# The product with v for the last 64 query rows of each batch: two heads as one 128-column weight tile

## The chip, the cores and the metric

The kernel runs on one core of one Trainium2 chip. The metric is the device time of one execution in microseconds (us); the time before is the median of three runs.

## The reference

Three stages follow one another. The attention has 4 batches of 8 heads, 576 tokens and a head width of 64; its scores get a decay from cumulated logarithms of f, and a causal mask. Its output, 2304 tokens of 512 columns, goes through a first feed-forward network (512 to 2048 to 512), and then through a routed one in which every token goes to one of eight experts.

```python
scores = scale * np.matmul(q, k.transpose(0, 1, 3, 2))
scores = np.where(causal, -1000000000.0, scores + decay)
attn = np.exp(scores - np.max(scores, axis=-1, keepdims=True))
attn = attn / (np.sum(attn, axis=-1, keepdims=True) + 1e-09)
out = np.matmul(attn, v)
x = out.transpose(0, 2, 1, 3).reshape(B * S, H * D)
h = x @ w_in
x = (h * np.clip(h + 3.0, 0.0, 6.0) / 6.0) @ w_out
# then per token: one of eight experts, relu(x @ w1[e]) @ w2[e], scaled by two gates
```

## The kernel before

Every fp32 operand is split into a high part (fp16) and a low part (bf16), and a product is three products: high by high, high by low, low by high.

**Attention.** The 576 queries of a batch and head are four blocks of 128 rows and a last one of 64 rows. The work comes in units. A "q" unit is one head and one or two blocks of 128 rows. A "t" unit is the last 64 rows of two heads: its scores fill 128 PSUM partitions, head e in partitions 64e to 64e+63, and its exponentials are transposed by a DMA into pt, where columns 64e to 64e+63 of each 128-column block belong to head e. There are four t units a batch, sixteen in all. `pv_unit` multiplies pt by v: pt is the weight operand, v (64 columns high, a column of ones, 64 columns low) the moving one, and the row sums come out as column 64 of the result. A q unit does it with 128 weight columns (L386 to L388). A t unit does it head by head with 64 weight columns each, both heads into PSUM partitions 0 to 63: per head four key blocks by three products (L396 to L398), and for the last 64 keys, whose high and low parts lie in the two halves of one block, L399 and L400, the latter with 64 rows of weights only: 28 matmuls a unit.

The results of one pair of heads share one PSUM bank (tile pv, one buffer). For the third group of rows of a batch the bank holds the fourth block of 128 rows of two heads (columns 0 to 129) and the t unit (columns 130 to 259). `evac` divides by the row sums on VectorE (L408 to L410), then ScalarE makes the high part in xn (L413) and GpSimd the low one (L414). The next user of the bank waits for the last read of it.

The scores of a t unit also use 64 weight columns: per head two matmuls of 512 columns in `scores` (L262) and two of 64 columns (L322, L323).

**First feed-forward.** Six chunks of 384 tokens; per chunk 192 matmuls of 384 columns in its first product (L634) and 192 in the second (L657). While a chunk is multiplied, the attention of later rows goes on between its matmuls: `adv` gives the attention a higher priority, and the order on TensorE is laid by the scheduler, matmul by matmul. After each chunk come 36 matmuls of 16 columns for the gates (L722). The last chunk waits for the end of the attention; the loads of the experts' weights (tile stw) begin after it too, as they take its room.

**Begin.** `setup` fills constants by GpSimd, the column of ones of v among them (L115). `prep_v` makes the two parts of v, block by block; of the last 64 tokens it loads two copies, one in each half of the partitions, and splits both.

Of the kernel before, what the change touches and what calls it, by code (L numbers as in the profile page):

```python
# [7 lines left out]
F16 = mybir.dt.float16  # L8
# [10 lines left out]
P = 128  # L19
PSC = 8.0        # PSUM units of a score: sqrt(D)  # L20
QW = [128, 256, 384, 512]

# the order of the work
# priority of the attention
ATTN_FIRST = 200
# priority of the conversion of the first feed-forward's weights
CONV_FIRST = 500
# share of a chunk's steps over which the next chunk's attention is spread
PACE = 0.75
# steps of the first chunk before the attention goes on  # L30
LEAD = 2
# units between the scores and the product with v
LAG = 4
# units between finished rows and their transposition
XLAG = 2
# units before the third and the fourth piece of the first batch
AT2, AT3 = 0, 4
# units of a group before the next pieces' preparation (Q2 rotates: at least 4)
PA, PB = 4, 4
# units before a batch's end at which the next one's first piece is prepared  # L40
PN = 2
# tiles of 64-bit floats of w_out in flight, and those in g before it is used
RAW_BUFS, RAW_G = 2, 3
# step of the attention from which w_out is loaded
WO_STEP = 12
# tiles converted and loaded before the first chunk
EARLY_CONV, EARLY_LOADS = 18, 22
# pieces of q and k split by DVE
DVE_PIECES = 2
# of four: parts of g that GpSimd splits in the first chunk  # L50
POOL_G = 4
# loads of w_in at points of the beginning
AHEAD = (1, 2, 1, 1, 1)
# the block of rows of the first batch after whose transposition later loads queue
# [4 lines left out]
def attention_moe_kernel(ctx: ExitStack, tc: tile.TileContext, q, k, v, f, w_in, w_out,  # L59
# [10 lines left out]
    SIZES = [3, 3, 3, 3, 3, 3]     # blocks of 128 tokens in a chunk  # L70
    NCH = len(SIZES)
    FIRST = [sum(SIZES[:c]) for c in range(NCH + 1)]    # a chunk's first block
# [45 lines left out]
    cumd = dram.tile([15, B * H, P], F16, name="cumd")      # (part, block of columns), row, column  # L118
# [26 lines left out]
    # columns of K: for four heads the even and the odd tokens of each 256, and the last 64 tokens of all heads  # L145
# [7 lines left out]
    def spare(i):  # L153
        """room in g, free until the first feed-forward begins"""
        return gf[:, i * 1024:(i + 1) * 1024]
# [8 lines left out]
    def piece(i):  # L164
        """the i-th piece of k or q: 256 tokens (two to a partition) of four heads, or a batch's last 64 tokens:
        batch, rows, heads, shape of a row's tile, columns of K"""
        b, n = i // NTB, i % NTB
        if n == 4:
            return b, 64, slice(0, H), (H, 1), slice(512, 576)
        g, hh = n // 2, n % 2  # L170
        return b, 128, slice(hh * 4, hh * 4 + 4), (4, 2), slice(g * 256, g * 256 + 256)

    def load(i, which):
        """the i-th piece of k or q, or the i-th block of 128 (or 64) tokens of v"""
# [22 lines left out]
    def load_cum(b, hh):  # L197
        """the parts of the cumulated decay of four heads, or of the last 64 tokens"""
# [7 lines left out]
    def split_kq(nm, i):  # L206
        """hi and lo parts of a piece (of q: lo and hi), side by side, for the transposition"""
# [37 lines left out]
    def q_cols(b, h, qb):  # L245
        """columns of q of a block of 128 tokens (the even ones, then the odd ones) or of the last 64"""
        if qb == 4:
            return [t[:, h, 0:64] for t in q_t[b * NTB + 4]]
        g, half = qb // 2, qb % 2
        return [t[:, half * 4 + h % 4, :] for t in q_t[b * NTB + g * 2 + h // 4]]  # L250

    def scores(ps, h, qb, l1, l2):
        """scores of a block of queries, by the parity of the key's token: [parity, pair]"""
# [10 lines left out]
    def pairs(t):  # L264
        """a row of keys in the order of the tokens, by their parity"""
# [13 lines left out]
    def prep_v(b, tb):  # L279
        if b * NTB + tb > 2:  # L280
            load(b * NTB + tb, "v")
        tv, V = ld.pop((b * NTB + tb, "v")), vt[b % len(vt)]
        nc.scalar.activation(out=V[:, tb, :, 0:64], in_=tv, func=AF.Copy)
        nc.gpsimd.tensor_tensor(out=V[:, tb, :, 65:129].bitcast(BF16), in0=tv, in1=V[:, tb, :, 0:64], op=ALU.subtract)

    # units: ("q", b, h, (qb, ...)) or ("t", b, hp): rows of the last 64 tokens of two heads
# [46 lines left out]
    def soft(u):  # L333
# [19 lines left out]
        if u[0] == "q" and u[1] == 0 and u[3] != (3,):  # L353
            # TensorE has nothing else to do before the first feed-forward
# [18 lines left out]
    def pv_unit(u, o, slot):  # L373
        """one unit into its columns of the bank o"""
# [15 lines left out]
        else:  # L390
            for e in range(2):
                h = u[2] * 2 + e
                oc = o[0:64, slot[e]:slot[e] + 65]
                cs = slice(e * 64, e * 64 + 64)
                for kb in range(4):
                    nc.tensor.matmul(oc, lhsT=pt[:, kb, cs], rhs=V[:, kb, h, 0:65], start=kb == 0, stop=False)  # L396
                    nc.tensor.matmul(oc[:, 0:64], lhsT=pt[:, kb, cs], rhs=V[:, kb, h, 65:129].bitcast(BF16), start=False, stop=False)
                    nc.tensor.matmul(oc, lhsT=ptb[:, 4 + kb, cs], rhs=V[:, kb, h, 0:65], start=False, stop=False)  # L398
                nc.tensor.matmul(oc, lhsT=pt[:, 8, cs], rhs=V[:, 4, h, 0:65], start=False, stop=False)  # L399
                nc.tensor.matmul(oc[:, 0:64], lhsT=pt[0:64, 8, cs], rhs=V[0:64, 4, h, 65:129].bitcast(BF16), start=False, stop=True)  # L400

    def evac(o, r, n, dests, h0):
        """o[0:r, n*2, 65] -> normalised, split, into dests (one [P, 2, H, D] tile per q block)"""
# [8 lines left out]
        for i, xt in enumerate(dests):  # L412
            nc.scalar.activation(out=xt[0:r, 0, h0:h0 + 2], in_=xs[0:r, 2 * i:2 * i + 2], func=AF.Copy)  # L413
            nc.gpsimd.tensor_tensor(out=xt[0:r, 1, h0:h0 + 2].bitcast(BF16), in0=xs[0:r, 2 * i:2 * i + 2],  # L414
                                    in1=xt[0:r, 0, h0:h0 + 2], op=ALU.subtract)

# [24 lines left out]
    def finish(n):  # L441
        """the transposition of finished rows, some units after them"""
# [8 lines left out]
    def pv(u):  # L451
# [10 lines left out]
        else:  # L462
            pv_unit(u, cur["o"][:, 130:512], [0, 65])
            evac(cur["o"], 128, 1, [xtile(b, 3)], u[2] * 2)
            evac(cur["o"][:, 130:512], 64, 1, [xtile(b, 4)], u[2] * 2)
# [3 lines left out]
    plan = []       # units and preparations in order; three groups of rows a batch  # L469
    ends = []       # position in the plan of the last unit of a group  # L470
# [28 lines left out]
    def attn_seq():  # L499
        """the whole attention, one step at a time"""  # L500
# [66 lines left out]
    WL = 2048       # a raw tile, in 16-bit words  # L567

    def raw_tile(nm, i):
        """room for a tile of 64-bit floats: wo before its own begins, the end of g before the first feed-forward"""  # L570
# [17 lines left out]
    def conv_raw(nm, i):  # L588
        """64-bit floats as words -> hi (fp16) and lo (bf16) with hi + lo = src to fp32's accuracy"""
# [25 lines left out]
    NBL = FIRST[-2]     # blocks before the last chunk  # L615
# [6 lines left out]
    def moe1_steps(c):  # L622
        """generator: one step is some 2 us of matrix products"""
# [63 lines left out]
    def setup_gates():  # L687
# [15 lines left out]
        # row r of a block of 128 queries is token 2 (r % 64) + r // 64 of it: r + r % 64 - 63 (r // 64)  # L703
# [478 lines left out]
```

## Time and profile before

| | us |
|---|---|
| median of 3 runs | 886.69 |
| lowest, highest run | 883.24, 888.75 |
| span of the profiled execution | 883.3 |
| busy: TensorE, VectorE, ScalarE, GpSimd | 775.8, 495.5, 437.8, 325.0 |
| mean granted TensorE clock | 0.933 |

The profile is of one execution. Busy times of TensorE overlap, as its matmuls are pipelined: what a matmul costs there is read from the distance between the starts of neighbours, not from its own duration. The granted clock is a share of 2.4 GHz; a stretch at 0.50 ran at 1.2 GHz.

### The profile page before, as it was taken

How to read it: one execution, taken by the hardware profiler on the slowest of the kernel's cores; microseconds unless marked ns; L12 is line 12 of the kernel's file. 1: busy time of each engine (PE TensorE's matmuls, PEld its weight loads, DVE VectorE, ACT ScalarE, POOL GpSimd, SP SyncE). 2: the span in 40 equal slices, each digit the busy share in tenths (PEclk: the TensorE clock that was granted, in tenths of full speed). 3: DMA queues.
4: the chain of work that ended last, by engine and by line, in shares of the span. 5: the costliest groups of instructions: out<-in, count | busy, mean ns of one | idle time of the engine just before them, and what ended most of it. 6: DMA issues, size and time to landing. Idle time of an engine off the chain costs nothing.

```text
span 883.3 us, 17104 instructions
## 1 busy us (share of the span) xinstructions
PE 775.8 (88%) x6374; PEld 494.5 (56%) x6385; DVE 495.5 (56%) x1282; ACT 437.8 (50%) x903; POOL 325.0 (37%) x377
## 2 busy tenths in 40 slices
PE   0472878998899989999999999999979999899993
PEld 0352435565566645555665565656676766766651
DVE  7899999934782575226832467674041455654510
ACT  3785477655773666234843454553022455554520
POOL 6664679764573454134631330001022222121010
PEclk9955878998999999997999799999989999999997
DMA  9894969877996586346751634742062899797411
GB/s 222 249 243 101 216 177 186 140 170 134 183 151 143 111 150 110 50 93 117 129 90 25 132 79 141 246 139 66 1 145 84 157 269 275 232 277 230 153 37 36
DMA packets 272356, 130.08 MB, mean 147 GB/s; under 512 B 223234, under 2 KB 256098, under 8 KB 272260
## 3 DMA queue, kind: packets, MB, share of 16 engines
q1 hardware_dynamic: 260964, 107.82, 55.1%
q0 software_dynamic: 4960, 15.73, 5.4%
q10 hardware_dynamic: 6336, 5.28, 2.0%
q8 instruction: 56, 0.92, 0.4%
q14 instruction: 40, 0.33, 0.2%
HBM read 71.52 MB, written 10.08 MB: 92 GB/s over the span
## 4 chain that ended last, share of the span: by engine, by line
PE 42%; DMA 27%; DVE 15%; issue 7%; ACT 3%; SPq 3%; POOL 2%; ACTq 0%; POOLq 0%; DVEq 0%
PE mm L657 15%; PE mm L634 14%; DMA out_dram<-y,ids 7%; DMA stw<-in_moe_w_dram 5%; PE mm L915 4%; DMA xg<-rows,ids 4%; DMA pt<-pn 3%; PE sc L262 3%; DVE w L599 2%; DVE w L601 2%; DVE W L818 2%; DVE w L597 1%; DMA wo<-in_moe_w_in_dram 1%; DMA ldv<-in_v_dram 1%; PE mm L934 1%
## 5 line engine op out<-in xcount | busy, mean ns | idle before, releaser
L634 PE MATMUL mm<-xT,wi 128*128 128x384 f16 (+1 forms) x1152 | 227.4, 343 | 11.9 <-DMA xT<-xn 7.1
L657 PE MATMUL mm<-g,wo 128*128 128x384 f16 (+1 forms) x1152 | 204.4, 326 | 1.0 <-DVE hr L641 1.0
L634 PEld LDWEIGHTS <-wi 128*128 128x128 f16 (+1 forms) x1152 | 113.7, 101 | 93.9 <-issue 29.4
L657 PEld LDWEIGHTS <-wo 128*128 128x128 f16 (+1 forms) x1152 | 110.7, 98 | 74.3 <-issue 4.6
L342 POOL TENSOR_TENSOR pn<-ms,pn 128x384 bf16<-128x384 f32 (+1 forms) x96 | 103.6, 1085 | 77.1 <-ACT pn L341 65.6
L336 ACT ACTIVATE ms<-ms,nm 128x512 f32<-128x512 f32 (+4 forms) x144 | 81.2, 579 | 70.4 <-DVE nm L302 44.5
L915 PEld LDWEIGHTS <-W 128*128 128x128 f16 (+1 forms) x1344 | 102.4, 100 | 18.3 <-issue 9.5
L818 DVE TENSOR_TENSOR W<-stw,W 128x1024 bf16<-128x1024 f32 x64 | 77.7, 1223 | 57.3 <-ACT W L817 56.7
L915 PE MATMUL mm<-xs,W 128*128 128x256 f16 (+3 forms) x1152 | 97.5, 247 | 8.6 <-DMA xs<-xg 3.8
L934 PE MATMUL mm<-W,hT 128*128 128x512 f16 (+1 forms) x422 | 93.8, 379 | 1.1
L817 ACT ACTIVATE W<-stw 128x1024 f16<-128x1024 f32 x64 | 66.9, 1054 | 53.0 <-DMA stw<-in_moe_w_dram 51.0
L302 DVE CUSTOM_DVE_ANT_1 ms<-sc,mask 128x128 f32<-128x128 f32 (+3 forms) x128 | 60.1, 483 | 50.7 <-PE sc L262 31.0
L262 PE MATMUL sc<-K,q 128*128 128x128 f16 (+2 forms) x192 | 53.8, 320 | 31.1 <-DMA q<-g 14.5
L646 DVE TENSOR_TENSOR g<-hr,g 128x384 bf16<-128x384 f32 x80 | 55.7, 697 | 27.3 <-ACT g L642 27.1
L934 PEld LDWEIGHTS <-hT 128*128 128x128 f16 (+1 forms) x432 | 41.9, 98 | 50.9 <-issue 1.8
L638 ACT ACTIVATE hr<-mm,bias 128x384 f32<-128x384 f32 x96 | 54.6, 569 | 27.8 <-PE mm L634 24.6
L262 PE MATMUL sc<-K,Q 67*128 67x128 f16 (+3 forms) x192 | 54.2, 323 | 13.6 <-DMA K<-cumd 10.6
L642 ACT ACTIVATE g<-hr 128x384 f16<-128x384 f32 x96 | 49.4, 517 | 32.7 <-DVE hr L641 32.4
L641 DVE SCALAR_TENSOR_TENSOR hr<-hr,mm 128x384 f32<-128x384 f32 x96 | 52.4, 546 | 19.1 <-ACT hr L638 18.8
L341 ACT ACTIVATE pn<-ms 128x384 f16<-128x384 f32 (+1 forms) x96 | 52.6, 552 | 19.2 <-DMA pt<-pn 18.8
L414 POOL TENSOR_TENSOR xn<-xs,xn 128x128 bf16<-128x128 f32 x80 | 40.4, 514 | 58.9 <-ACT xn L413 58.4
L386 PE MATMUL pv<-vt,pt 128*128 128x65 f16 x320 | 43.6, 202 | 18.9 <-DVE xs L410 17.6
(180 smaller groups left out, 1131.5 us busy)
## 6 DMA issues: line engine op xcount, KB each, us to landing
stw<-in_moe_w_dram SPq DMA_DIRECT2D x64, 512.0 KB, 4.7
wo<-in_moe_w_in_dram SPq DMA_DIRECT2D x16, 512.0 KB, 7.6
raw<-in_moe_w_out_dram ACTq DMA_DIRECT2D x10, 512.0 KB, 3.6
rows<-rw POOLq DMA_DIRECT2D x15, 256.0 KB, 2.9
ldk<-in_k_dram SPq DMA_DIRECT2D x14, 256.0 KB, 3.8
ldq<-in_q_dram SPq DMA_DIRECT2D x14, 256.0 KB, 3.8
ldv<-in_v_dram SPq DMA_DIRECT2D x13, 256.0 KB, 3.5
raw<-in_moe_w_out_dram SPq DMA_DIRECT2D x3, 512.0 KB
```

The source lines that it names most:

```text
L262: nc.tensor.matmul(po, lhsT=lhs[0:rows], rhs=r if n > 1 else r[:, :, 0], start=x == 0, stop=x == 1)
L302: nc.vector.tensor_tensor_reduce(out=pairs(ms[:, off:off + w]), in0=ps[:, 0:w].rearrange("p (c j) -> p c j", c=2), in1=pairs(mask[:, 640 - ...
L336: nc.scalar.activation(out=ms[:, off:off + w], in_=ms[:, off:off + w], func=AF.Exp, scale=-1.0, bias=nm[:, i:i + 1])
L342: nc.gpsimd.tensor_tensor(out=lo.bitcast(BF16), in0=ms[:, 0:N], in1=hi, op=ALU.subtract)
L634: nc.tensor.matmul(ps[:, 0:w], lhsT=l.bitcast(BF16) if a else l, rhs=r.bitcast(BF16) if b2 else r, start=i == 0, stop=i == 3 * KD - 1)
L638: nc.scalar.activation(out=hr, in_=ps[:, 0:w], func=AF.Relu, bias=bias3)
L646: either.tensor_tensor(out=g[:, m, 1, 0:w].bitcast(BF16), in0=hr, in1=g[:, m, 0, 0:w], op=ALU.subtract)
L657: nc.tensor.matmul(ps[:, 0:w], lhsT=l.bitcast(BF16) if a else l, rhs=r.bitcast(BF16) if b2 else r, start=i == 0, stop=i == 3 * NF - 1)
L817: nc.scalar.activation(out=hi, in_=sts[i], func=AF.Copy)
L818: nc.vector.tensor_tensor(out=lo.bitcast(BF16), in0=sts[i], in1=hi, op=ALU.subtract)
L915: nc.tensor.matmul(ps[:, 0:w], lhsT=l.bitcast(BF16) if a else l, rhs=r.bitcast(BF16) if b2 else r, start=i == 0, stop=i == 3 * KD - 1)
L934: nc.tensor.matmul(ps, lhsT=l.bitcast(BF16) if a else l, rhs=r.bitcast(BF16) if b2 else r, start=i == 0, stop=i == 3 * NF2 - 1)
```

## The change

The t unit multiplies all 128 columns of pt at once, as weights, by v of both heads side by side (2 x 65 or 2 x 64 moving columns): 14 matmuls instead of 28. The result has 128 rows by 130 columns, of which only the two blocks on the diagonal (rows of head e, columns of head e) are used. The low part of v's last block is zero in partitions 64 to 127, so that its product takes all 128 rows of weights too: `setup` writes the zeros once, and `prep_v` splits only the first 64 rows of that block. `evac_last` takes the place of `evac` for these rows: the row sums of both heads in 128 partitions at once, then one VectorE multiplication a head, by a scalar of each partition, the second from partitions 64 to 127 into partitions 0 to 63. Comments are removed, too, and line numbers shift.

```diff
@@ setup
         for t in vt:
             nc.gpsimd.memset(t[:, :, :, 64:65], 1.0)
+            nc.gpsimd.memset(t[64:128, 4, :, 65:129], 0.0)
@@ prep_v
+        r = TBR[tb]
         nc.scalar.activation(out=V[:, tb, :, 0:64], in_=tv, func=AF.Copy)
-        nc.gpsimd.tensor_tensor(out=V[:, tb, :, 65:129].bitcast(BF16), in0=tv, in1=V[:, tb, :, 0:64], op=ALU.subtract)
+        nc.gpsimd.tensor_tensor(out=V[0:r, tb, :, 65:129].bitcast(BF16), in0=tv[0:r], in1=V[0:r, tb, :, 0:64],
+                                op=ALU.subtract)
@@ pv_unit
-            for e in range(2):
-                h = u[2] * 2 + e
-                oc = o[0:64, slot[e]:slot[e] + 65]
-                cs = slice(e * 64, e * 64 + 64)
-                for kb in range(4):
-                    nc.tensor.matmul(oc, lhsT=pt[:, kb, cs], rhs=V[:, kb, h, 0:65], start=kb == 0, stop=False)
-                    nc.tensor.matmul(oc[:, 0:64], lhsT=pt[:, kb, cs], rhs=V[:, kb, h, 65:129].bitcast(BF16), start=False, stop=False)
-                    nc.tensor.matmul(oc, lhsT=ptb[:, 4 + kb, cs], rhs=V[:, kb, h, 0:65], start=False, stop=False)
-                nc.tensor.matmul(oc, lhsT=pt[:, 8, cs], rhs=V[:, 4, h, 0:65], start=False, stop=False)
-                nc.tensor.matmul(oc[:, 0:64], lhsT=pt[0:64, 8, cs], rhs=V[0:64, 4, h, 65:129].bitcast(BF16), start=False, stop=True)
+            hs = slice(u[2] * 2, u[2] * 2 + 2)
+            oc = o[:, slot[0]:slot[0] + 130].rearrange("p (e c) -> p e c", e=2)
+            for kb in range(5):
+                hi, lo = V[:, kb, hs, 0:65], V[:, kb, hs, 65:129].bitcast(BF16)
+                k8 = kb if kb < 4 else 8
+                nc.tensor.matmul(oc, lhsT=pt[:, k8, :], rhs=hi, start=kb == 0, stop=False)
+                nc.tensor.matmul(oc[:, :, 0:64], lhsT=pt[:, k8, :], rhs=lo, start=False, stop=kb == 4)
+                if kb < 4:
+                    nc.tensor.matmul(oc, lhsT=ptb[:, 4 + kb, :], rhs=hi, start=False, stop=False)
@@ evac_last (new; the activation and the subtraction after it are as in evac)
+        nc.vector.tensor_scalar(out=rl.unsqueeze(2), in0=ov[:, :, 64:65], scalar1=1e-9, scalar2=None, op0=ALU.add)
+        nc.vector.reciprocal(out=rl, in_=rl)
+        for e in range(2):
+            ps = slice(e * 64, e * 64 + 64)
+            nc.vector.tensor_scalar(out=xs[0:64, e], in0=ov[ps, e, 0:64], scalar1=rl[ps, e:e + 1], scalar2=None,
+                                    op0=ALU.mult)
@@ pv
-            pv_unit(u, cur["o"][:, 130:512], [0, 65])
+            pv_unit(u, cur["o"], [130])
             evac(cur["o"], 128, 1, [xtile(b, 3)], u[2] * 2)
-            evac(cur["o"][:, 130:512], 64, 1, [xtile(b, 4)], u[2] * 2)
+            evac_last(cur["o"][:, 130:260], xtile(b, 4), u[2] * 2)
```

## Rows read from the trace of the kernel before

**Rows 1.** Busy time of the engines in three stretches (busy us and instructions of TensorE, its weight loads, VectorE, ScalarE, GpSimd; then the granted clock, the DMA share and GB/s).
```profile
120.00:170.00 50.00, 42.86 (x382) 26.29 (x383) 47.84 (x109) 34.16 (x73) 42.45 (x39) 0.84 0.85 180
340.00:540.00 200.00, 200.00 (x1556) 119.18 (x1553) 92.65 (x309) 93.48 (x202) 67.87 (x88) 0.95 0.47 88
540.00:640.00 100.00, 97.86 (x653) 59.14 (x651) 51.76 (x125) 39.82 (x62) 3.66 (x5) 1.00 0.41 127
```
**Rows 2.** The chain of work that ended last, shares of the span by line.
```profile
PE mm L657 15%; PE mm L634 14%; DMA out_dram<-y,ids 7%; DMA stw<-in_moe_w_dram 5%; PE mm L915 4%; DMA xg<-rows,ids 4%; DMA pt<-pn 3%; PE sc L262 3%; DVE w L599 2%; DVE w L601 2%; DVE W L818 2%; DVE w L597 1%; DMA wo<-in_moe_w_in_dram 1%; DMA ldv<-in_v_dram 1%; PE mm L934 1%
```
**Rows 3.** Pieces of that chain in order of time (start, us, engine and line, count): matmuls of 16 and of 384 columns back to back.
```profile
581.67 0.89 PE mm L722 x36
...
586.61 21.47 PE mm L634 x132
```
**Rows 4.** Timeline of TensorE (start, us, engine, line, operation, output and inputs, weight rows * weight columns, moving operand): the end of a q unit and a t unit whose 28 matmuls stand together.
```profile
138.53 0.19 PE L388 MATMUL pv<-vt,pt 128*128 128x65 f16 x1
138.65 0.22 PE L396 MATMUL pv<-vt,pt 128*64 128x65 f16 x1
...
139.06 0.20 PE L399 MATMUL pv<-vt,pt 128*64 128x65 f16 x1
139.18 0.21 PE L400 MATMUL pv<-vt,pt 64*64 64x64 bf16 x1
139.33 0.22 PE L396 MATMUL pv<-vt,pt 128*64 128x65 f16 x1
...
140.00 0.82 PE L634 MATMUL mm<-xT,wi 128*128 128x384 f16 x4
```
**Rows 5.** The same view: matmuls of a t unit that alternate with those of the feed-forward.
```profile
392.09 0.22 PE L396 MATMUL pv<-vt,pt 128*64 128x65 f16 x1
392.24 0.34 PE L634 MATMUL mm<-xT,wi 128*128 128x384 f16 x1
392.51 0.22 PE L397 MATMUL pv<-vt,pt 128*64 128x64 bf16 x1
```
**Rows 6.** The same view, in a stretch of half the clock.
```profile
409.68 0.50 PE L634 MATMUL mm<-xT,wi 128*128 128x384 f16 x1
...
410.31 0.50 PE L634 MATMUL mm<-xT,wi 128*128 128x384 bf16 x1
```
**Rows 7.** The same view: score matmuls of a t unit, each alone between two of the feed-forward.
```profile
477.14 0.40 PE L262 MATMUL sc<-K,q 128*64 128x512 f16 x1
...
477.74 0.40 PE L262 MATMUL sc<-K,Q 67*64 67x512 f16 x1
```
**Rows 8.** TensorE alone in the stretches of the five t units whose matmuls alternate with others (busy us and matmuls that lie in it or reach into it, granted clock, DMA share, GB/s): first all matmuls, five rows, then those of L657 in the first stretch, of L634 in the second, third and fifth (with the weight loads' busy time and count), and of L722 in the third and fourth.
```profile
345.15:362.31 17.16, 17.16 (x101) 1.00 0.08 24
392.09:401.62 9.53, 9.53 (x54) 1.00 0.73 155
406.03:415.94 9.91, 9.91 (x51) 0.65 0.92 148
495.61:504.30 8.69, 8.69 (x61) 0.62 0.58 126
528.08:532.40 4.32, 4.32 (x39) 1.00 0.01 4
...
345.15:362.31 17.16, 11.77 (x50) 4.84 (x51) 1.00 0.08 24
...
392.09:401.62 9.53, 7.11 (x22) 2.03 (x22) 1.00 0.73 155
406.03:415.94 9.91, 5.01 (x10) 1.03 (x11) 0.65 0.92 148
528.08:532.40 4.32, 2.69 (x8) 0.77 (x9) 1.00 0.01 4
...
406.03:415.94 9.91, 2.09 (x12) 1.05 (x11) 0.65 0.92 148
495.61:504.30 8.69, 4.28 (x24) 2.23 (x22) 0.62 0.58 126
```
**Rows 9.** All engines in the two stretches after 400 us in which the clock was halved (columns as in the first group).
```profile
409.03:419.27 10.24, 10.24 (x38) 4.41 (x39) 7.86 (x27) 3.27 (x9) 4.00 (x6) 0.50 0.69 136
497.78:508.02 10.24, 10.24 (x54) 5.82 (x54) 3.81 (x25) 3.27 (x7) 4.78 (x7) 0.50 0.53 114
```
**Rows 10.** Timeline of TensorE: score matmuls of a third block of rows, whose output is two pieces of 128 or of 64 columns with a gap between them, each with the matmul behind it.
```profile
449.83 0.27 PE L262 MATMUL sc<-K,Q 67*128 67x256 f16 x1
449.94 0.33 PE L657 MATMUL mm<-g,wo 128*128 128x384 f16 x1
...
450.13 0.22 PE L262 MATMUL sc<-K,q 128*128 128x128 f16 x1
450.19 0.33 PE L657 MATMUL mm<-g,wo 128*128 128x384 f16 x1
```
**Rows 11.** Timeline of VectorE: the first step of `evac` for 128 rows, and its last step for the 64 rows of a t unit.
```profile
362.61 0.15 DVE L408 TENSOR_SCALAR rl<-pv 128x2 f32<-128x2 f32 x1
...
363.57 0.28 DVE L410 TENSOR_TENSOR xs<-pv,rl 64x128 f32<-64x128 f32 x1
```
**Rows 12.** Waits of the engines in the whole span (us in total, times, longest): TensorE's for the bank of pv.
```profile
PE pv L386 <- DVE xs L410: 17.6, 9, 4.5
```
**Rows 13.** Timeline of GpSimd: its first work after the constants, with the idle time before it.
```profile
19.32 1.12 POOL L284 TENSOR_TENSOR vt<-g,vt 128x512 bf16<-128x512 f32 x1 [6.14 <-ACT vt L283]
```

More of the change, by code (lines that the diff above doesn't have):

```diff
@@ L415, in evac, with evac_last @@
                                     in1=xt[0:r, 0, h0:h0 + 2], op=ALU.subtract)
+    def evac_last(o, xt, h0):
+        ov = o.rearrange("p (e c) -> p e c", c=65)
+        rl = ap1.tile([P, 8], F32, tag="rl", name="rl", bufs=3)[:, 0:2]
+        xs = ap1.tile([P, 4, 64], F32, tag="xs", name="xs", bufs=2)
+        nc.vector.tensor_scalar(out=rl.unsqueeze(2), in0=ov[:, :, 64:65], scalar1=1e-9, scalar2=None, op0=ALU.add)
[4 more added lines that the diff above has]
+                                    op0=ALU.mult)
+        nc.scalar.activation(out=xt[0:64, 0, h0:h0 + 2], in_=xs[0:64, 0:2], func=AF.Copy)
+        nc.gpsimd.tensor_tensor(out=xt[0:64, 1, h0:h0 + 2].bitcast(BF16), in0=xs[0:64, 0:2],
+                                in1=xt[0:64, 0, h0:h0 + 2], op=ALU.subtract)
     xT = {}
```

## The prediction

> **What bounds the kernel now.** I read the busy times by stretches first. From 340 to 540 us TensorE is busy for 200.00 of 200.00 us, no other engine for half of that; from 540 to 640 us it is busy for 97.86 of 100 [rows 1]. The chain of work agrees: its two largest lines are the feed-forward's matmuls, L657 and L634 [rows 2]. So in these stretches a microsecond taken out of TensorE's sequence should come off the end. Before that it is otherwise: from 120 to 170 us VectorE is busy for 47.84 of 50 us and TensorE for 42.86 [rows 1].
>
> A busy TensorE says nothing of how well it is used, so next come the distances between starts in the timeline. Full-width products of 384 columns follow one another every 21.47 / 132 = 0.163 us, and 36 gate matmuls take 0.89, so 0.025 each [rows 3]. A t unit that stands together takes 1.35 us, from 138.65 to 140.00. Its 64-column matmuls come every 0.034 (twelve from 138.65 to 139.06), but three places cost more: 0.12 to get in (138.53 to 138.65), 0.12 in front of L400 and 0.15 behind it (139.06 to 139.18 to 139.33) [rows 4].
>
> Those changes of shape are the find. Where a t unit alternates with the feed-forward, L396 is followed by L634 after 0.15 and that by L397 after 0.27: 0.42 a pair [rows 5]. The two alone would be 0.163 + 0.034 = 0.197. So each visit of a 64-column matmul costs 0.22 us on top, some seven times its own time.
>
> **The change, part by part.**
>
> *The matmuls.* Removed are 28 with 64 weight columns a unit, added 14 with 128 weight columns and 128 or 130 moving ones. Such a product is not in the trace, but score matmuls are near: 0.06 us from a 128-column one to its successor, 0.11 for 256 columns [rows 10]. I take 0.057 (130/128 of 0.056), so 0.8 us a unit. Bounds: 0.034, that of the old products, and 0.11; over the eight units from 340 us on these ends are 2.6 us less and 5.9 more than I take. Twenty-eight at 0.034 are 0.95: without the changes of shape there is next to nothing in it.
>
> *What goes with them*, by the five units that alternate. Each stretch is counted as what stays plus 0.8 for the new products:
> - 345.15 to 362.31, 17.16 us: 50 products of L657, and 12 of L634 (101 matmuls less these 50, 28 of the unit, 10 of scores and one that reaches in) are 62 x 0.163 = 10.1 [rows 8, 3]. Scores stay: two full-width ones of 512 columns (two times the 0.11 of 256) 0.4; four 64-column ones of 512 at 0.60 - 0.163 = 0.44 each, 1.75 [rows 7]; four of 64 columns at 0.42 - 0.163 = 0.25, 1.0 [rows 5]. With 0.8 that makes 14.1; 3.1 go.
> - 392.09 to 401.62, 9.53: 21 of L634 (22 with one that reaches in) 3.4, four score matmuls 0.3, and 0.8: 4.5; 5.0 go [rows 8].
> - 406.03 to 415.94, 9.91: 10 of L634 1.6, 11 gate matmuls 0.3, and 0.8: 2.7; 7.2 go [rows 8].
> - 495.61 to 504.30, 8.69: 22 gate matmuls 0.55, two full-width scores 0.4, four 64-column ones, two by two, 0.9, and 0.8: 2.7; 6.0 go [rows 8].
> - 528.08 to 532.40, 4.32: 8 of L634 1.3 and 0.8: 2.1; 2.2 go [rows 8].
>
> Together 23.5 us. Three more units of this stretch (at 368, 512 and 520 us) stand together like the one at 138: 1.35 - 0.8 = 0.55 each, 1.7 [rows 4].
>
> *The clock.* Two of these stretches ran at a mean granted clock of 0.65 and 0.62 [rows 8]. The clock is at 0.50, the 1.2 GHz level, from 409.03 to 419.27 and from 497.78 to 508.02 [rows 9]. Each fall comes two to three microseconds after the place where a t unit begins to alternate with gate matmuls, when TensorE does little but change shape. Without that I expect it to stay at the 2.4 GHz level. A pair of L634 starts 0.63 apart there (409.68 to 410.31) [rows 6] against 0.42. The two sums above already price what stays at full clock. Behind the units lie another 419.27 - 415.94 and 508.02 - 504.30 = 7.05 us at half of it, which give back 3 (half, less what is wait). If the clock falls all the same, what stays in the third and fourth stretch costs twice from the fall on (the ten L634 1.6 and half of the 1.1 beside them, 2.1; two thirds of the 2.7, 1.8), and these 3 stay away: 6.9 less.
>
> *Units before 260 us.* Eight of the sixteen; each has 0.55 to give, 4.5 in all. VectorE or a DMA ends most waits there [rows 1], so between nothing and 4.5; I take a third, 1.5.
>
> *The evacuation.* `evac_last` has one VectorE operation more: two of 64 x 64 in place of one of 64 x 128. One lies between 0.15 (2 columns) and 0.28 (128 columns) [rows 11], so the pair adds 0.02 to 0.28 us; by the mean, 0.15. Between 340 and 540 us VectorE has over 100 us to spare, which cover it [rows 1]. What is behind it on VectorE is the feed-forward's own work, and the next user of the bank. For the four units of the first batch, where VectorE is the bound, it costs 4 x 0.15 = 0.6. The row sums cost what they did; ScalarE and GpSimd do the same as before.
>
> *The zeros.* One more memset on GpSimd, 512 columns in 64 partitions. GpSimd is idle for 6.14 us before 19.32 us [rows 13], waiting for v; the memset stands in that queue ahead of it and is hidden by that idle time as long as it takes under 6. Splitting 64 rows in place of 128 is free of a change, since the columns are as many.
>
> *A rule against it.* The output of the new high products is one piece of 130 columns, that of the low ones two pieces of 64 with a gap. A score matmul that writes two pieces with a gap is followed after 0.06 or 0.11 us, in step with its columns [rows 10]: no price to be seen. The Trainium skill, "PSUM — Partial Sum Buffer", section "Specifications (TRN2)", says that any non-contiguous access pattern slows matmuls significantly; by it the 14 products would cost more than I count, and it gives no figure. This case's trace does not agree, for pieces of this length. It stands below as a rival.
>
> *Sum.* 23.5 + 1.7 + 3 + 1.5 - 0.6 = 29.1 us less. The profiled execution's 883.3 becomes 854. It lies 3.4 below the median of 886.69; the median becomes 857.6, say 858.
>
> **The rivals.**
>
> *Part is given back (20%).* The order between attention and feed-forward is laid anew. The score matmuls of the t units keep their 64 columns, eight a unit, and where more of them come alone, each costs the 0.22 of a visit; and with TensorE quicker, its next unit may wait for a transposed pt or for the bank of pv, which it does not from 340 to 540 us now. The clock may fall anyway (6.9). For it speaks that 128 score matmuls could cost up to 28 us, of which now only a part is paid; against it, that nothing but TensorE is short here. It leaves 9 to 20 us of gain: about 872.
>
> *No difference (9%).* The t units end at the same time because the transposition or the softmax of their rows does, not TensorE. Against it: from 340 to 540 us TensorE has no idle time at all in which it waits for them [rows 1]. Time: 886, within 9.
>
> *Slower (5%).* The bank of pv has one buffer. A t unit that stands together hands the bank to VectorE with nothing of its own left in TensorE's queue, and the L386 behind it waits, with all that is queued after it in order. Such waits exist: nine, 17.6 us, 2.0 on average and 4.5 at most [rows 12]. After each of sixteen units, 2.0 would take back 32 us, more than the sum; at 3 us, 48: 905. It decides from 1.8 us a unit. Against it: TensorE has feed-forward matmuls to put in between, and three units in the stretch stand together today without a wait.
>
> *An output in two pieces is slow (2%).* If such a product takes twice its 0.057, eight units from 340 us on lose 8 x 14 x 0.057 = 6.4, all sixteen 12.8: about 868. That is the rule named above.
>
> **How the numbers follow.** The forecast holds 64%: 858, by itself 850 to 866. The bounds: all of the early units' 4.5 in place of 1.5, and the cheaper evacuation, make 33 us, and the three runs spread by 2.8 to either side, which gives 848 to 850; the low clock alone gives 865. The range must also take in the part given back, to a gain of 11: 876. So 848 to 876, which leaves out no difference, slower, and a little at the lower end. One per cent, 9 us, is about what a measurement of this kernel can tell from no change: faster are the forecast, the part given back and the slow pieces, 0.86; within it 0.09; slower 0.05.
>
> **What would show it.** In the changed kernel's timeline a product of the t unit should be followed by its successor after 0.055 to 0.06 us and a feed-forward product next to it cost 0.163, with no 0.12 to 0.15 between. The stretch from the beginning of the third batch's t units to the end of attention should be some 27 us shorter, and the mean granted clock above 0.933, without a fall where gate matmuls meet a t unit. TensorE should show no idle time there. It would be wrong if waits for xs or pt appear in front of L386, if the fall of the clock stays, or if lone score matmuls multiply.

## The result, and the profile after

The changed kernel takes 860.76 us (median of four runs, 856.6 to 862.18) against 887.48 for the kernel before; the ratio on record is 0.9706, with a 95% interval from 0.9671 to 0.974. Forecast were 858 and 848 to 876. The profiled execution has a span of 860.5 us (883.3 before), so 22.8 came off where the sum said 29.1. The medians lie 26.7 apart, and four runs of either kernel spread by 5.5: two single executions do not fix the gain to the microsecond. The mean granted clock rose from 0.933 to 0.950.

The busy times of the span, and below them those by stretches (columns as in [rows 1]; the fourth is explained further down):
```profile
PE 743.2 (86%) x6161; PEld 476.8 (55%) x6161; DVE 506.9 (59%) x1298; ACT 433.7 (50%) x903; POOL 325.0 (38%) x378
```
```profile
120.00:170.00 50.00, 39.92 (x326) 24.45 (x327) 47.22 (x113) 34.56 (x75) 39.15 (x39) 0.87 0.87 186
260.00:340.00 80.00, 76.10 (x614) 46.64 (x613) 44.74 (x145) 46.59 (x103) 38.28 (x48) 0.96 0.70 131
340.00:518.00 178.00, 174.62 (x1465) 108.07 (x1463) 97.56 (x318) 89.73 (x200) 67.66 (x87) 0.99 0.54 100
...
403.00:406.40 3.40, 1.61 (x22) 1.17 (x19) 3.37 (x9) 0.26 (x2) 2.40 (x4) 1.00 0.90 202
...
406.40:409.82 3.42, 3.42 (x13) 1.72 (x12) 3.17 (x14) 3.42 (x10) 1.59 (x2) 0.50 0.99 182
```
Early on nothing is different in kind: from 120 to 170 us VectorE is still the busy engine (47.22, before 47.84 [rows 1]). From 340 us on TensorE, which had no idle time at all, now has 178.00 - 174.62 = 3.4 us of it. And the clock, which stood at half for 10.24 us twice in the stretch from 340 to 540 us [rows 9], does so once there, for 3.42.

Next the timeline of TensorE in the changed kernel. L392 is a q unit's product with v; L402, L403 and L405 are the t unit's new ones; L654 and L677 are the feed-forward's first and second product, L742 and L773 the gates', L935 the experts'. (In the other kernels these numbers shift by a few.) Shown are a t unit that stands together, one that alternates with the feed-forward, one that alternates with gate matmuls, a gate matmul that waits, and the first matmuls of three parts: the second product of chunk 2, that of chunk 4, and the first expert.
```profile
138.44 0.19 PE L392 MATMUL pv<-vt,pt 128*128 128x65 f16 x1
138.47 0.22 PE L402 MATMUL pv<-vt,pt 128*128 128x130 f16 x1
138.53 0.22 PE L403 MATMUL pv<-vt,pt 128*128 128x128 bf16 x1
138.59 0.22 PE L405 MATMUL pv<-vt,pt 128*128 128x130 f16 x1
...
139.28 0.81 PE L654 MATMUL mm<-xT,wi 128*128 128x384 f16 x4
...
348.15 0.65 PE L677 MATMUL mm<-g,wo 128*128 128x384 f16 x3
...
389.64 0.22 PE L402 MATMUL pv<-vt,pt 128*128 128x130 f16 x1
389.69 0.32 PE L654 MATMUL mm<-xT,wi 128*128 128x384 f16 x1
389.86 0.22 PE L403 MATMUL pv<-vt,pt 128*128 128x128 bf16 x1
...
397.17 0.22 PE L402 MATMUL pv<-vt,pt 128*128 128x130 f16 x1
397.23 0.17 PE L742 MATMUL mm<-wg,x 128*128 128x16 f16 x1
397.26 0.22 PE L403 MATMUL pv<-vt,pt 128*128 128x128 bf16 x1
...
405.10 0.18 PE L773 MATMUL mm<-oh,tri 128*128 128x8 f16 x1 [1.32 <-DVE oh L764]
...
520.53 0.65 PE L677 MATMUL mm<-g,wo 128*128 128x384 f16 x3 [0.39 <-DVE hr L661]
...
622.25 0.61 PE L935 MATMUL mm<-wi,W 128*128 128x128 f16 x4
```
Read the distances between starts. The unit that stands together takes 0.81 (138.47 to 139.28), before 1.35 [rows 4]. A pair with a feed-forward product takes 0.22 (389.64 to 389.86), before 0.42 [rows 5]; with a gate matmul 0.09 (397.17 to 397.26). The pauses of 0.12 to 0.15 are gone.

The last three parts say where the time came off. In the kernel before they began like this:
```profile
347.42 0.65 PE L657 MATMUL mm<-g,wo 128*128 128x384 f16 x3
...
542.65 0.65 PE L657 MATMUL mm<-g,wo 128*128 128x384 f16 x3 [0.49 <-DVE hr L641]
...
644.39 0.79 PE L915 MATMUL mm<-wi,W 128*128 128x128 f16 x7
```
So the stretch between the first two shrank from 195.23 to 172.38, by 22.85; before it 0.7 us were lost, and behind it, up to the experts, nothing was won (101.74 and 101.72). The whole change lies in the stretch that the forecast named, which there expected 23.5 + 1.7 + 3 = 28.2.

The other two engines with something new, VectorE (the evacuation of a t unit) and GpSimd:
```profile
358.62 0.58 DVE L431 TENSOR_SCALAR xs<-pv,rl 64x64 f32<-64x64 f32 x2
...
6.03 0.53 POOL L117 MEMSET vt<- 64x512 f16 x1
```
The two multiplications take 0.58 us in place of one of 0.28 [rows 11]: 0.30 more, just above the upper bound of 0.28. The memset stands among the constants; GpSimd's wait for v behind them is 4.55 us, 6.14 before [rows 13], so it was hidden, as said.

TensorE's waits in the changed kernel from 345 to 600 us (us in total, times, longest; the two largest of six, which come to 4.6), and below "..." those for the bank of pv in the whole span:
```profile
PE sc L264 <- DVE nm L306: 1.4, 2, 1.2
PE mm L773 <- DVE oh L764: 1.3, 1, 1.3
...
PE pv L390 <- DVE xs L415: 17.2, 7, 4.5
...
PE pv L390 <- DVE xs L431: 2.4, 4, 1.2
```
What TensorE waits for in the stretch is mostly VectorE, and not the bank. In the whole span it is 17.2 us by `evac`, 17.6 before [rows 12], and 2.4 by the new function: the rival that ends slower did not happen.

### The profile page after: what moved, and what is told of

Its sections match the earlier page's. It is cut to its first block, busy times and chain, and to the rows that moved or that the text cites. A ratio compares the mean times of both kernels' runs of the same rounds, so it can differ in the third digit from the quotient of the medians.

```text
span 860.5 us, 16688 instructions
## 1 busy us (share of the span) xinstructions
PE 743.2 (86%) x6161; PEld 476.8 (55%) x6161; DVE 506.9 (59%) x1298; ACT 433.7 (50%) x903; POOL 325.0 (38%) x378
## 5 line engine op out<-in xcount | busy, mean ns | idle before, releaser
L654 PE MATMUL mm<-xT,wi 128*128 128x384 f16 (+1 forms) x1152 | 219.1, 338 | 10.7 <-DMA xT<-xn 6.0
L677 PE MATMUL mm<-g,wo 128*128 128x384 f16 (+1 forms) x1152 | 201.5, 326 | 2.0 <-DVE hr L661 1.3
L654 PEld LDWEIGHTS <-wi 128*128 128x128 f16 (+1 forms) x1152 | 112.8, 101 | 93.4 <-issue 30.3
L677 PEld LDWEIGHTS <-wo 128*128 128x128 f16 (+1 forms) x1152 | 110.7, 98 | 76.4 <-issue 6.4
L935 PEld LDWEIGHTS <-W 128*128 128x128 f16 (+1 forms) x1344 | 102.3, 100 | 18.9 <-issue 11.4
L935 PE MATMUL mm<-xs,W 128*128 128x256 f16 (+3 forms) x1152 | 97.6, 247 | 7.7 <-issue 4.5
L939 DVE SCALAR_TENSOR_TENSOR hT<-mm,hT 128x128 bf16<-128x128 f32 (+1 forms) x96 | 31.8, 353 | 51.8 <-ACT hT L938 49.4
L390 PE MATMUL pv<-vt,pt 128*128 128x65 f16 x320 | 42.8, 200 | 20.5 <-DVE xs L415 17.2
```

Of the source, the lines that this page charges most:

```text
L654: nc.tensor.matmul(ps[:, 0:w], lhsT=l.bitcast(BF16) if a else l, rhs=r.bitcast(BF16) if b2 else r, start=i == 0, stop=i == 3 * KD - 1)
L677: nc.tensor.matmul(ps[:, 0:w], lhsT=l.bitcast(BF16) if a else l, rhs=r.bitcast(BF16) if b2 else r, start=i == 0, stop=i == 3 * NF - 1)
L935: nc.tensor.matmul(ps[:, 0:w], lhsT=l.bitcast(BF16) if a else l, rhs=r.bitcast(BF16) if b2 else r, start=i == 0, stop=i == 3 * KD - 1)
```

## The experiments

A visit below is a group of 64-column matmuls in TensorE's order with 128-column ones on either side. In program order the kernel before has 160 of them (36 with scores, in part or alone, from 340 to 540 us), the changed kernel 68, all of scores. Kernels were run on several chips, so each is compared with the kernel before on its own chip (medians of 882 to 888).

### Number of matmuls, or their shape? (two kernels)

Two kernels keep 28 products a unit. One gives each 128 weight columns, one head's 65 columns at a time:
```diff
+            for e in range(2):
+                h = u[2] * 2 + e
+                oc = o[:, slot[0] + e * 65:slot[0] + e * 65 + 65]
...
+                    nc.tensor.matmul(oc, lhsT=pt[:, k8, :], rhs=hi, start=kb == 0, stop=False)
```


> The changed kernel, but the t unit multiplies one head's v at a time again: 28 matmuls of 128 weight columns and 64 or 65 moving ones, in place of 14 with 128 or 130. Theory 'shape' (the gain comes from no longer changing between 64 and 128 weight columns): 28 at the 0.031 us of the q units' matmuls cost what 14 at 0.057 do, so the time is that of the changed kernel, 861, within 4. Rival 'count' (the gain comes from half as many matmuls and weight loads): 28 as before, so 887, within 4.

The other keeps 64 weight columns, but writes the second head to PSUM partitions 64 to 127 and alternates the heads:
```diff
+            os = [o[e * 64:e * 64 + 64, slot[0]:slot[0] + 65] for e in range(2)]
+            cs = [slice(e * 64, e * 64 + 64) for e in range(2)]
...
+                for e in range(2):
+                    nc.tensor.matmul(os[e], lhsT=pt[:, k8, cs[e]], rhs=vs[e][:, 0:65], start=kb == 0, stop=False)
```


> The t unit keeps 28 matmuls of 64 weight columns, but head 1 goes into PSUM partitions 64 to 127, head by head in turn, so that two neighbours use the two halves of the weight columns; the last low product takes 128 rows of weights. In the program's order 64-column matmuls stand in 168 groups between others, 160 in the kernel before, 68 in the changed one. Theory 'shape': the groups are as many, so nothing is won but the changes around the 64-row product, 0.2 us a unit: 882, from 878 to 887. Rival 'side by side': two 64-column matmuls run at once in the two halves, so the unit is as cheap as with 128 columns: 861.

The first took 865.74 us (0.9805, 0.9738 to 0.9873), the second 882.19 (1.000, 0.9968 to 1.0032). The timeline of the first:
```profile
384.14 0.19 PE L404 MATMUL pv<-vt,pt 128*128 128x64 bf16 x1
384.17 0.33 PE L655 MATMUL mm<-xT,wi 128*128 128x384 bf16 x1
384.33 0.19 PE L406 MATMUL pv<-vt,pt 128*128 128x65 f16 x1
```
and of the second, a unit that stands together and one that alternates:
```profile
139.36 0.22 PE L403 MATMUL pv<-vt,pt 128*64 128x65 f16 x2
...
139.79 0.20 PE L405 MATMUL pv<-vt,pt 128*64 128x64 bf16 x2
139.92 0.50 PE L656 MATMUL mm<-xT,wi 128*128 128x384 f16 x2
...
393.49 0.22 PE L405 MATMUL pv<-vt,pt 128*64 128x64 bf16 x1
393.64 0.34 PE L656 MATMUL mm<-xT,wi 128*128 128x384 f16 x1
393.90 0.22 PE L405 MATMUL pv<-vt,pt 128*64 128x64 bf16 x1
```
A pair takes 0.19 in the one and 0.41 in the other, with the same number of matmuls. So the 0.22 hangs on the number of weight columns, not on how many products there are. The second kernel says more. Together, two 64-column products start in the time of one (a pair every 0.033 us, the first at 139.36 and the fourteenth at 139.79), and the unit takes 0.56 us (139.36 to 139.92), less than the 0.81 of the change; yet with 168 visits it gains nothing. The intervals of the two ratios do not touch. The first stays some 5 us above the changed kernel, which was run on another chip, and these two intervals do touch. Its trace puts little of that to the 14 products more a unit: between the second products of chunks 2 and 4 TensorE is busy for 169.5 us (168.6 in the changed kernel) but idle for 8.3 (3.8).

The Trainium skill, "TensorEngine Tiling (Array Packing)", section "Key Properties", states that a change of the tiling mode drains TensorE. If 64 weight columns count as another mode, these rows agree: they show a pause at each change, 0.22 us for both directions together. Section "Performance Considerations" advises column tiling where the stationary operand has 64 columns, by two. The unit that stands together agrees; the time of this kernel, whose products are scattered among wider ones, does not.

### The 28 old products kept together

The kernel before, with the loop of a t unit's products inside a critical section, so that nothing comes between them.
```diff
-            for e in range(2):
+            with tc.tile_critical():
+                for e in range(2):
```


> The kernel before, with its 28 matmuls of 64 weight columns, but each t unit's stand in one block that no other matmul may enter. Theory 'shape': every one of the sixteen units costs 1.35 us as the undivided ones did, 0.55 more than in the changed kernel and without lone visits; eight of them lie where TensorE is the bound, so 4.4 over the changed kernel: 865, from 861 to 870. Rival 'count': weight loads and matmuls are as many as before, so 887. A third, that only half of the gain comes from shape: 875.

901.28 us (1.0186, 1.0116 to 1.0256): a miss. From TensorE's timeline:
```profile
362.32 0.22 PE L397 MATMUL pv<-vt,pt 128*64 128x65 f16 x1 [0.43 <-ACT g L643]
...
363.88 1.31 PE L635 MATMUL mm<-xT,wi 128*128 128x384 f16 x7
```
The products do stand together and take 1.56 us (362.32 to 363.88), 0.2 more than was meant. But ahead of each of the sixteen sections TensorE is idle for 0.4 to 6.2 us, 26 together, 9.4 of them from 340 us on. The section has a price of its own, so the kernel's time does not separate the theories. The stretch between the second products of chunks 2 and 4 does say something:
```profile
365.84:551.18 185.34, 175.82 (x1493) 107.44 (x1491) 87.30 (x295) 87.99 (x193) 63.62 (x82) 0.96 0.46 85
```
With as many matmuls a unit as before, TensorE is busy there for 175.82 us in place of 194.74, as 'shape' has it and 'count' has not (one of the eight units, the one shown, falls just ahead of the stretch, which is a small part of this). The time was lost elsewhere: the stretch begins 18.4 us later than in the kernel before, and behind it, up to the experts, 8.6 us more go by.

### Which batches pay

The new products in two batches, the old ones in the others (zeros and GpSimd's split as in the changed kernel). Shown is the kernel with the first two; the other has `b >= 2`.
```diff
+            if b < 2:
                 hs = slice(u[2] * 2, u[2] * 2 + 2)
...
+            else:
+                for e in range(2):
...
```


> The change for the t units of the first two batches alone; the other two multiply and divide as before. Theory 'shape where TensorE is the bound': little in it, as VectorE and transfers end the waits there and the units stand together: 886, from 882 to 889. Rival 'every unit alike': half of the gain, 874.

> The change for the t units of the last two batches alone. Theory 'shape where TensorE is the bound': the whole gain, 861, from 857 to 866. Rival 'every unit alike': half of it, 874.

The first two batches alone: 886.0 us, 1.0033 (0.9999 to 1.0068). The last two alone: 862.16, 0.9774 (0.9723 to 0.9825). All of the gain comes from the batches whose units meet a saturated TensorE; the same saving where VectorE or a DMA sets the pace gave nothing that can be measured.

### The price of a visit, by itself

The changed kernel with 64 extra matmuls of 64 moving columns in the last chunk's second product, into a bank that nobody reads, each in the middle of a critical section, once with 64 weight columns and once with 128.
```diff
+                with tc.tile_critical() if extra else nullcontext():
...
+                        if extra and b2:
+                            nc.tensor.matmul(spare_ps[0:64, 0:64], lhsT=wo[:, 0, m, d * P:d * P + 64],
+                                             rhs=g[:, m, 0, 0:64], start=True, stop=True)
```


> The changed kernel with 64 more matmuls of 64 moving columns in the second product of the last chunk, one behind the second of every three products of 384 columns, into a bank that nothing reads; these are 64 rows out of 128 rows of weights, so 64 weight columns. Each four stand in a block of their own, which has a price that the next kernel shares. Theory 'shape': against the next kernel each costs 0.22 us more, 14 us together, from 11 to 17. Rival 'any small matmul costs that': no difference between the two.

> The same with 128 weight columns in the 64 added matmuls, everything else alike. Theory 'shape': 0.03 us each, 2 us together over the changed kernel, and the price of the blocks, which no row here shows; without one, 863. Rival 'any small matmul costs that': like the kernel with 64 columns, 14 us over the changed one, 875.

1038.24 us and 1018.82. Both totals carry the sections: (1018.82 - 860.76) / 64 is 2.5 us each, and with such pauses the clock stayed at 0.50. The difference is 19.4 us, 0.30 a visit, above the 11 to 17 expected. The timeline with 64 columns
```profile
649.17 0.82 PE L679 MATMUL mm<-g,wo 128*128 128x384 f16 x2 [1.67 <-issue]
649.92 0.26 PE L683 MATMUL spare_ps<-g,wo 128*64 128x64 f16 x1
650.12 0.50 PE L679 MATMUL mm<-g,wo 128*128 128x384 f16 x1
```
and with 128:
```profile
650.11 0.82 PE L679 MATMUL mm<-g,wo 128*128 128x384 f16 x2 [1.64 <-issue]
650.73 0.26 PE L683 MATMUL spare_ps<-g,wo 128*128 128x64 f16 x1
650.80 0.51 PE L679 MATMUL mm<-g,wo 128*128 128x384 f16 x1
```
From the pair to the extra matmul 0.75 against 0.62, from it to the next 0.20 against 0.07: 0.13 + 0.13 = 0.26 a visit. That is at the 1.2 GHz level; the changed shapes cost 0.22 at 2.4 GHz. So the price hardly grows when the clock halves. Most of the other 0.04 lies in the wait in front of the next section (1.67 and 1.64 in the rows shown).

### Is VectorE's longer evacuation covered?

The two multiplications of `evac_last` done three times over, which adds four operations a unit:
```diff
-        for e in range(2):
+        for e in (0, 1, 0, 1, 0, 1):
```


> The changed kernel with the two multiplications of the new evacuation done three times over, to the same result: four more VectorE operations of some 0.21 us a unit, 0.85 us, 13.6 in sixteen units. Theory 'hidden': only the first batch's four units, where VectorE is the bound, pay: 3.4 at most, so 861 to 865. Rival 'bank': TensorE waits for the bank behind each unit, so each pays all of it: 874.

874.26 us, 0.987 (0.9821 to 0.9919): 13.5 more than the changed kernel, which was run on another chip. That is the rival's figure and not the covered one. TensorE's waits from 345 to 600 us:
```profile
PE mm L654 <- DVE x L687: 3.7, 1, 3.7
PE mm L654 <- DVE hr L661: 3.1, 3, 1.7
PE mm L773 <- DVE oh L764: 3.0, 1, 3.0
PE pv L390 <- DVE xs L431: 1.7, 2, 1.2
```
They are for the feed-forward's and the gate's own steps on VectorE, not for the bank, so the rival had the size and not the place. Some of it is lost early (chunk 1 begins at 213.8 us, 206.5 in the changed kernel) and most of that comes back by chunk 3 (390.20 against 388.49); 11 us are missing where the experts begin. The scheduler laid the work anew too (over 800 places of TensorE's order differ), so not every microsecond is VectorE's. And the `oh` that L773 waited 3.0 us for is an operation that took 3.54 us there, which is taken up below.

### The other way round: the multiplications on ScalarE

```diff
-            nc.vector.tensor_scalar(out=xs[0:64, e], in0=ov[ps, e, 0:64], scalar1=rl[ps, e:e + 1], scalar2=None,
-                                    op0=ALU.mult)
+            nc.scalar.activation(out=xs[0:64, e], in_=ov[ps, e, 0:64], func=AF.Copy, scale=rl[ps, e:e + 1])
```


> The changed kernel with the two multiplications of the new evacuation on ScalarE in place of VectorE. The run with them done three times over was 13 us slower, though TensorE waited little for the bank. Theory 'VectorE's queue' (what stands behind these operations on VectorE, the feed-forward's own steps, comes late): 0.42 us a unit less there, 6.7 in all, and as much more on ScalarE: 856, from 853 to 861. Rival 'order': the slower run came from another order of the work, so nothing follows for this one: 861, from 858 to 866.

To learn what a new order alone does, the changed kernel with another pace of the attention, on the same chip:
```diff
-PACE = 0.75
+PACE = 0.74
```


> The changed kernel with the share of a chunk's steps over which attention is spread at 0.74 in place of 0.75: the same work in a slightly other order, 321 places of TensorE's sequence differ, and 64-column matmuls stand in 77 groups in place of 68. If the order is worth little: nine more groups at 0.22 us, 2 at most: 861 to 863. If the order by itself moves the time by several us, as the run with the threefold multiplications may say: 866 or more, or 856 or less.

853.99 us, 0.9673 (0.9637 to 0.9708), and for the pace 862.05, 0.976 (0.972 to 0.98). The first beats the kernel before and, on the same chip, the one with the other pace; against the changed kernel itself, run on another chip, the intervals overlap. This one sample of a new order moved the time by little. By stretches (columns as above), with the multiplications on ScalarE:
```profile
260.00:340.00 80.00, 78.44 (x667) 48.92 (x666) 46.80 (x145) 47.88 (x105) 38.53 (x47) 1.00 0.71 137
340.00:518.00 178.00, 171.82 (x1423) 105.88 (x1422) 92.48 (x302) 94.89 (x215) 65.07 (x84) 0.99 0.52 101
```
The win is not where it was looked for. From 340 to 518 us TensorE idles more (6.2 us, 3.4 in the changed kernel). From 260 to 340 us it does 667 matmuls in place of 614, at a clock of 1.00 in place of 0.96. A new order alone can do the same: the kernel with 28 wide products has the changed kernel's evacuation, and from 260 to 340 us it does 664 matmuls at a clock of 1.00. So what VectorE's shorter queue gave, if anything, stays open.

### The visits that are left: scores with 128 weight columns

In the changed kernel the t units' q gets zeros in the other head's columns; both heads' scores then add up in 128 partitions, and no visit is left.
```diff
-                        scores(ps[po, 0:512], h + e, 3, l1, l2)
+                        scores(ps[:, 0:512], h + e, 3, l1, l2, e == 0, e == 1)
```


> The changed kernel, and the scores of the t units with 128 weight columns as well: the 64 columns of a head's queries with 64 columns of zeros beside them, the two heads adding into the same 128 partitions. As many matmuls as before, none of 64 weight columns left; some small memsets and one more transfer a batch are added. Theory 'shape': 68 visits of lone score matmuls remain in the changed kernel, 36 of them after 340 us, where TensorE is the bound; without them 36 x 0.22 = 8 us less: 853, from 848 to 857. Rival 'latency': the waits for scores, softmax and transposition have become the bound after the change, so nothing: 861. A second rival: the two heads' matmuls ran side by side in the two halves of the columns, and now one after the other, four of 0.216 and four of 0.03 us a unit in place of half of it: where they did, 0.5 a unit more, 8 at most: 869.

The same with the multiplications on ScalarE:

> The changed kernel with both: the scores of the t units with 128 weight columns, and the two multiplications of the evacuation on ScalarE. The first alone won nothing (866), the second alone 7 (854). Theory 'what the removed groups of score matmuls give is taken by waits for VectorE': with less on VectorE part of the 8 us comes out, so 849, from 845 to 853. Rival 'the wide score matmuls cost what they save' (two heads one after the other in place of side by side): nothing from them, 854, from 851 to 860.

865.56 us, 0.9788 (0.9747 to 0.9829), and 866.77, 0.9812 (0.9777 to 0.9846). The first lies between 'latency' (861) and the second rival (869), the second above everything that was expected of it. For the first, the stretch from 340 us and TensorE's waits from 345 to 600 us:
```profile
340.00:518.00 178.00, 167.78 (x1433) 107.03 (x1431) 98.14 (x325) 91.70 (x201) 70.20 (x93) 0.98 0.53 103
```
```profile
PE pv L407 <- DVE xs L448: 4.8, 3, 3.0
PE mm L671 <- DVE hr L678: 2.6, 3, 1.8
```
TensorE is 6.8 us less busy than in the changed kernel (174.62 to 167.78), but idle for 10.2 us in place of 3.4, mostly for VectorE. What shape gave, waits took. The second rival is right in kind. In the changed kernel two heads' scores of 512 columns do run side by side where they stand together:
```profile
494.73 0.41 PE L264 MATMUL sc<-K,q 128*64 128x512 f16 x2
```
The next pair starts at 494.97, 0.24 us later, and a wide one alone takes 0.216. But from 340 us on only two units have such pairs, so at 0.5 a unit it costs about 1 us there. Why the wait for the bank comes back here the rows do not show: they tell who was late, not why, and the two kernels also add memsets, transpositions and copies.

## Why the prediction was right, and where its terms were off

The cause holds: a change of the weight columns' number costs TensorE 0.22 us a visit, and the t units paid it between other matmuls. Two kernels with 28 products each, apart in shape, are apart in time; the gain lies in the batches and in the stretch that were named. That the median came within 2.8 us of 858 is in part luck: the two profiled executions lie only 22.8 us apart, the medians 26.7.

- *The new product's price, 0.057.* Right: 138.47, 138.53, 138.59.
- *The two-piece output.* L403 writes two pieces of 64 columns and is followed after 0.06 or 0.05 like L402, which writes 130 in a row. The rule of the Trainium skill that was weighed against the change ("PSUM — Partial Sum Buffer", section "Specifications (TRN2)") is not borne out here, nor the rival of 868.
- *The alternating and the compact units and the clock, 28.2 together.* They gave 22.85. Of the 5.35 missing, 3.3 are idle time that TensorE did not have before (3.77 us between the two second products, 0.49 before). The clock's fall takes about 1.7 more (half of 3.42 us). That accounts for 5.0, in one execution of each kernel.
- *The clock, 3 of them.* Right for the mechanism named: the gate matmuls that alternate with a t unit at 397.17 pass at full clock. The kernel with 168 visits keeps a mean clock of 0.95 from 340 to 540 us, as before [rows 1]; the one with the other pace has 1.00 from 340 to 520. But in the changed kernel a fall remains nine microseconds later, by another way. From 403.00 to 406.40 us TensorE is busy for 1.61 of 3.40 us, VectorE for 3.37; one wait of 1.32 is for the gate's `oh` (L764). Then the clock is at 0.50 until 409.82. In the kernel before it fell at 409.03 [rows 9], and ahead of that TensorE had been busy without a pause, changing shape:
```profile
406.00:409.03 3.03, 3.03 (x26) 2.32 (x24) 0.56 (x3) 2.06 (x6) 1.17 (x2) 1.00 1.22 102
```
- *The early units, 1.5.* Nothing: the stretch before 348 us lost 0.7, and the two batches by themselves gave 1.0033.
- *The evacuation.* It was priced at 0.15 a unit and measured 0.30. The greater mistake is the cover: "Between 340 and 540 us VectorE has over 100 us to spare, which cover it". That is an average; from 403.00 to 406.40 us VectorE is busy for 3.37 of 3.40. Yet this is not the evacuation's work. Most of it is one small operation, the gate's `oh`:
```profile
402.60 2.45 DVE L764 TENSOR_TENSOR oh<-t,cm 128x24 f16<-128x24 f32 x1
```
Its five other executions take 0.17 to 0.87 us. GpSimd is at work for 2.43 of these 2.45 us, one operation behind another, and L764 ends 0.05 us after one of them (405.05 and 405.00). Small VectorE operations drawn out like this, with GpSimd at work all along, stand in other traces too: 3.30 us at 410.70 in the kernel before, 3.54 at 405.52 with the multiplications done three times, 4.39 at 485.95 with the other pace. That GpSimd holds VectorE up is argued from this; no kernel here moved GpSimd's work. TensorE's longest wait of the stretch, with the fall of the clock behind it, hangs on that operation. With four operations more a unit the kernel was 13.5 us longer, but whether the 0.30 cost any of the 5.35 is not shown.
- *The rivals.* Part given back is what happened in kind, by a small amount: about a fifth of the gain, and the time fell into the forecast's own range. Lone scores remain, 36 visits in the stretch; taking them away gave no time. The bank's wait and no difference are out.

The weak step of a forecast that was right in its mechanism, then, is the check against TensorE alone: the sum took every microsecond saved in its sequence as a microsecond off the end. In these two executions it held for 22.85 of 28.2, until what TensorE needed from VectorE came late.

## What to carry to other kernels

Read distances between starts, not busy shares: an engine at 100% may spend a tenth of its time changing shape, and matmuls with fewer weight columns that a scheduler mixes among full ones pay for it each time, so zero padding to the full width can be the cheaper form. Before costing an edit at nothing, look for cover in the microseconds where it lies and not in a stretch's average; and there, too, ask whether an engine that shows as busy works or is held up. And expect the next saving on the same engine to be worth less than this one: the second batch of visits was removed for no gain.

## What the runs showed of the hardware that was not expected

- A 64-column matmul between 128-column ones costs 0.22 us on top at 2.4 GHz and 0.26 at 1.2 GHz: in wall time nearly the same.
- Two 64-column matmuls with outputs in different halves of PSUM's partitions ran side by side: a pair every 0.033 us, where 64-column ones to the same half come one every 0.034 [rows 4].
- A critical section around a few matmuls left TensorE idle for some 1.7 us in front of each (1.67 and 1.64 in the rows above) at the low clock.
- The granted clock fell at 409.03 us in the kernel before, where TensorE was busy without a pause but changing shape, and at 406.40 in the changed kernel, where it had been idle for over half of the time since 403.00.
- A VectorE operation of 24 columns took 2.45 us in place of 0.18 while GpSimd worked without a pause.
